# A sparse attention and feed-forward kernel: the first batch's feed-forward units pinned in traced order, at other rates, and its transposes one tile later

## The chip, the cores and the metric

The kernel runs on one core of a Trainium2 chip. The metric is the device time of one execution in microseconds (us); before the change the median of three runs is 1228.44 us (1227.75 to 1228.84). A core has five engines that work side by side, each on its own instructions in their fixed order: TensorE (PE in the profile) multiplies matrices and transposes, VectorE (DVE) and ScalarE (ACT) do element-wise work and reductions, GpSimd (POOL) more of that, and SyncE (SP) issues the transfers. A matrix product is accumulated in PSUM, a small memory of banks, from which DVE and ACT read it. TensorE's order comes from a list scheduler: the program is traced in Python, each instruction gets a priority by the place where it was traced, and for each engine the scheduler picks among the instructions that it believes ready.

## The reference

There are 8 batches of 8 heads, 576 positions, 64 values a head. Scores are thresholded at their row's maximum less tau, and the attention output feeds a two-layer unit with 512 inputs and 2048 hidden values.

```python
scores = scale * np.matmul(q, k.transpose(0, 1, 3, 2))
thresh = np.max(scores, axis=-1, keepdims=True) - tau
scores = np.where(scores >= thresh, scores, -1000000000.0)
attn = np.exp(scores - np.max(scores, axis=-1, keepdims=True))
attn = attn / (np.sum(attn, axis=-1, keepdims=True) + 1e-09)
x = np.matmul(attn, v)            # then heads side by side: 4608 rows of 512
h = x @ w_in
out = (h * (1.0 / (1.0 + np.exp(-h)))) @ w_out
```

## The kernel before

**Tiles.** Attention runs over tiles of 128 query rows. A tile's number t is in its names: `s_53` is the score tile 53 in PSUM, `w32_53` its weights, `hl_53` their split into a high and a low half-precision part. Batch 0 has tiles 0 to 15 (the first 256 rows of each head, "low") and 28 to 47 (the other 320 rows, "high"); numbers 16 to 27 are empty steps. Batch 1 has tiles 49 to 84, and from 85 on each batch has 36 tiles, up to 300. A tile goes through `scores` (TensorE, L452 in batch 0 and L464 later), `soft1` (DVE, row maximum, L474), `soft1b` (ACT, the exponential, L484), `soft2` (DVE, threshold and row sum, L493), `soft2b` (scaling by the sum: POOL at L507 in batch 0, ACT at L511 later) and `soft3`. The last differs. In batch 0, whose tiles stay in fp32, `soft3_direct` transposes five blocks on TensorE (L403 `tm`, L408 `tl`) and ACT copies them to `wT` (L416, L417). From batch 1 on POOL makes the two half-precision parts (L519, L522, L525), and a transfer transposes them (L535). When both heads of a pair have all tiles of a range in `wT`, `av_direct` (L426) or `av` (L550) multiplies by V, and `av_post` writes the result to `x16`.

**Buffers.** Two score tiles in PSUM, four `w32`, four `hl`, three `wT`. A `wT` buffer holds one head of one pair and range; batch 0 and the later batches share the three.

**Feed-forward units (FFN).** When a range of a batch is complete, `moe_units` adds its units to a list: 16 `h_unit`s (12 matmuls each, L593, then two steps on ACT and two on DVE at L601 to L609) and 16 quarters of `o_unit`s (12 matmuls each, L624; the fourth quarter of each writes its output by ACT and a transfer, L634 and L636). `h_0_256_3` is the fourth hidden block for batch 0 from row 256 on, `o_0_0_2` the third output block for batch 0 from row 0.

**What sets the order.** A loop over t traces the work of each step, with priorities for scores (`PRI_S`), the softmax and later AVs; `av_direct`, the loads and the units have none. A credit grows by `rate` at each step and pays for one unit of the list at a time. For batch 0 the rate is given by `RATES`; from batch 1 on it is the number of units on the list over the steps to the next range, times 0.95, so units left over from before are counted in. The weights are loaded, decoded and split on ACT, DVE and POOL during batch 0 (`W_PLAN`). Batch 1's V is scaled with a factor that goes through a small matmul on TensorE, `v1_ps`, traced at step 51 (L114 by way of `vscale`), before its first AV.

Of the kernel before, what the change touches and what calls it, by code (L numbers as in the profile page):

```python
# [30 lines left out]
LOAD = 5  # L31
AV_LAG = 3
GAP, GAP1 = 12, 1
RATES = (0.9, 0.9)
RATE = 0.95

W_PLAN = ((0, 0, 10, 13, 0), (16, 9, 22, 36, 0))
# [14 lines left out]
def attention_moe(  # L52
# [10 lines left out]
    nc = tc.nc  # L63
# [35 lines left out]
    for i in range(2):  # L99
        t = const.tile([P, S + 64], F32R, name=f"qstack{i}")  # L100
# [263 lines left out]
    direct = {}  # L364
    qzero = {}
    for kind, base, n in (("low", 4096, 256), ("high", 5120, 320)):
        for i in range(2):
            t = gbuf.bitcast(F32)[:, base + 2 * n * i : base + 2 * n * (i + 1)]
# [69 lines left out]
    tiles = []  # L438
# [74 lines left out]
    def soft3(t):  # L513
        if tiles[t][0] in direct:
            return soft3_direct(t)
        w = wtile.pop(t)
        hl = sb.tile([P, 9, P], F16, tag="hl", name=f"hl_{t}", bufs=4)
        fl = hl.rearrange("p j c -> p (j c)")
        nc.gpsimd.tensor_scalar(  # L519
            out=fl[:, 0:S], in0=w, scalar1=1.0, scalar2=1.0, op0=ALU.mult, op1=ALU.mult  # L520
        )
        nc.gpsimd.tensor_tensor(  # L522
            out=fl[:, 640:1152], in0=w[:, 0:512], in1=fl[:, 0:512], op=ALU.subtract
        )
        nc.gpsimd.tensor_tensor(  # L525
            out=fl[:, 576:640], in0=w[:, 512:576], in1=fl[:, 512:576], op=ALU.subtract
        )
        v, parts = tiles[t]
        kind = visits[v][2]
        base = VISITS[kind][2][0][0]  # L530
        for h, i, r0, n in parts:
            if (v, h) not in wT:
                wT[v, h] = sb.tile([P, 9, S], F16, tag="wT", name=f"wT_{v}_{h}", bufs=3)
            c = i * P - base
            nc.sync.dma_start_transpose(out=wT[v, h][:, :, c : c + n], in_=fl[r0 : r0 + n, :])  # L535
# [50 lines left out]
    def h_unit(b, c0, n, f, own=None):  # L586
        if f == 0:
            place_g(b, c0, n)
        ph = bank([P, 512], f"h_{b}_{c0}_{f}", own)
        k = 0  # L590
        for c in range(NK):
            for lo_w, lo_x in ((0, 0), (0, 1), (1, 0)):
                nc.tensor.matmul(  # L593
                    ph[:, :n], wi(c, f, lo_w), x16[b, lo_x][:, c, c0 : c0 + n],
                    start=(k == 0), stop=(k == 11),
                )
                k += 1

        def post():
            th = sb.tile([P, WID], F32, tag="th", name=f"th_{b}_{c0}_{f}", bufs=2)  # L600
            nc.scalar.activation(th[:, :n], ph[:, :n], AF.Tanh, scale=moe_sc[b][:, 0:1])  # L601
            nc.vector.scalar_tensor_tensor(  # L602
                out=ph[:, :n], in0=th[:, :n], scalar=1.0, in1=ph[:, :n],
                op0=ALU.add, op1=ALU.mult,
            )
            o = gbase[b, c0] + 2 * n * f
            g = gbuf[:, o : o + 2 * n].rearrange("p (r n) -> p r n", r=2)
            nc.scalar.activation(g[:, 0, :n], ph[:, :n], AF.Copy, scale=2.0**-14)  # L608
            nc.vector.scalar_tensor_tensor(  # L609
                out=g[:, 1, :n], in0=ph[:, :n], scalar=2.0**-14, in1=g[:, 0, :n],  # L610
                op0=ALU.mult, op1=ALU.subtract,
            )
            gt[b, c0, f] = g

        return post

    def o_unit(b, c0, n, d, quarter, own=None):
        if quarter == 0:
            po[b, c0, d] = bank([P, 512], f"o_{b}_{c0}_{d}", own)
        ps = po[b, c0, d]  # L620
        for f in range(4 * quarter, 4 * quarter + 4):
            g = gt[b, c0, f]
            for k, (lo_w, lo_g) in enumerate(((0, 0), (0, 1), (1, 0))):
                nc.tensor.matmul(  # L624
                    ps[:, :n], wo(f, d, lo_w), g[:, lo_g, :n],
                    start=(f == 0 and k == 0), stop=(f == NF - 1 and k == 2),
                )

        def post():
            if quarter < 3:  # L630
                return

            o = wst[:, NW + d % 2, :]
            nc.scalar.activation(o[:, :n], ps[:, :n], AF.Copy, scale=moe_sc[b][:, 1:2])  # L634
            c = b * S + c0
            nc.sync.dma_start(out=outT[d * P : (d + 1) * P, c : c + n], in_=o[:, :n])  # L636

        return post
# [34 lines left out]
    def at(t, f):  # L673
        todo.setdefault(t, []).append(f)

    avs = {}
    ready = []
    start = {}
    for v, (b, p, kind) in enumerate(visits):
        if b == 0 and kind == "high" and p == 0:  # L680
            tiles.extend([None] * GAP)
            first_high = len(tiles)
        if b == 1 and p == 0 and kind != "high":
            tiles.extend([None] * GAP1)
        ta, tb, ranges = VISITS[kind]
        u = len(tiles)
        start.setdefault((b, p), u)
        ha = b * H + 2 * p
        for i in ta:
            if i < 4:  # L690
                tiles.append((v, [(ha, i, 0, P)]))
            else:
                tiles.append((v, [(ha, 4, 0, D), (ha + 1, 4, D, D)]))
        last_a = len(tiles) - 1
        for i in tb:
            tiles.append((v, [(ha + 1, i, 0, P)]))
        last_b = len(tiles) - 1
        use_b = last_a if 4 in ta else last_a + 1
        if b == 0:
            at(u - LOAD, lambda v=v: load_direct(v))  # L700
            at(u - 2, lambda v=v: scale_direct(v))
            c0, n = ranges[0]
            avs.setdefault(last_b + AV_LAG, []).append((v, p, c0, n))
            if p == NPAIR - 1:
                ready.append((last_b + AV_LAG + 1, b, c0, n))
            continue
        for h, use, tl, last in ((ha, u, ta, last_a), (ha + 1, use_b, tb + [4] * (4 in ta), last_b)):
            at(use - LOAD, lambda v=v, h=h, tl=sorted(tl): load_qk(v, h, tl))
            at(use - 3, lambda h=h: split_k(h))
            at(use - 2, lambda h=h, tl=sorted(tl): split_q(h, tl))  # L710
        for j, (c0, n) in enumerate(ranges):
            avs.setdefault(last_b + AV_LAG + j, []).append((v, p, c0, n))
        if p == NPAIR - 1:
            for j, (c0, n) in enumerate(ranges):
                ready.append((last_b + AV_LAG + j + 2, b, c0, n))
# [63 lines left out]
    def live(t):  # L779
        return 0 <= t < NT and tiles[t] is not None  # L780

    scores(0)
    t = 0
    while t < NT + 8 or units or ready or held:
        while ready and ready[0][0] <= t:
            _, b, c0, n = ready.pop(0)
# [4 lines left out]
            if b == 0:  # L791
                rate = RATES[0 if c0 == 0 else 1]
        if held and not ready and not units and t >= NT + 8:
# [8 lines left out]
            soft2b(t - 1)  # L802
        if live(t):
            pri(PRI_SOFT1, lambda: soft1b(t))()
        if live(t - 1):
            soft3(t - 1)
        for f in todo.pop(t, []):
            f()
        credit += rate
# [7 lines left out]
        for v, p, c0, n in avs.pop(t, []):  # L817
            b = visits[v][0]
# [58 lines left out]
```

## Time and profile before

| | |
|---|---|
| three runs, median | 1228.44 us (1227.75 to 1228.84) |
| the profiled execution | 1225.66 us |
| its span | 1223.9 us |
| PE busy / weight loads | 1150.3 us (94%) / 899.2 us (73%) |
| DVE, ACT, POOL busy | 933.7, 796.4, 707.5 us |
| mean granted TensorE clock | 0.987 |
| matmuls of the FFN | 2 x 3072, 425.8 and 417.9 us busy |

The span is the time from the first to the last instruction; the execution's own time has 1.76 us around it. "Busy" is the time in which an engine works on at least one instruction; matmuls overlap, and their ends are modelled, so a busy TensorE is not one at its peak. A row of a group names line, engine, operation, what it writes and reads, its count, and its busy time and mean duration in ns; behind the last bar stands the engine's idle time ahead of it, and what ended that.

### The profile page before, as it was taken

Reading aid. Unit: us, or ns where it says so; the run is one execution under the profiler, and the core shown is the slowest. Engines: PE = TensorE matmul, PEld = TensorE weight load, DVE = VectorE, ACT = ScalarE, POOL = GpSimd, SP = SyncE. Lnnn points to the kernel's source line nnn. Section 1 sums busy time; section 2 is a strip of 40 time slices with the busy share of each in tenths; the row PEclk is TensorE's granted clock in tenths of the full one; section 3 lists DMA queues with packets and bytes.
Section 4 is the critical chain, followed back from the end, with each engine's and each line's share of the span. In section 5 each row is a group of like instructions: output and inputs, shape, how many; then the busy total and the mean of one; then the engine's idle time right before and its main releaser. Section 6 shows DMA issues by size and latency. Waiting matters only on the chain.

```text
span 1223.9 us, 27062 instructions
## 1 busy us (share of the span) xinstructions
PE 1150.3 (94%) x9474; PEld 899.2 (73%) x9474; DVE 933.7 (76%) x2625; ACT 796.4 (65%) x1505; POOL 707.5 (58%) x902
## 2 busy tenths in 40 slices
PE   6868799999899799999999999999999999999998
PEld 4545567777786577787777777788778877777777
DVE  7988988988999988889889858886788858333330
ACT  6667875876867777777777747785677756333331
POOL 2385357887877587886888428781778547100000
PEclk9979999999999999999999999999999999999999
DMA  9553148889788777886987448772877356200000
GB/s 309 185 161 95 41 108 173 160 160 177 132 177 141 160 137 139 150 165 151 167 149 145 114 94 155 146 136 82 153 150 142 77 92 116 42 11 16 16 10 25
DMA packets 340887, 151.73 MB, mean 124 GB/s; under 512 B 305936, under 2 KB 317200, under 8 KB 340752
## 3 DMA queue, kind: packets, MB, share of 16 engines
q1 hardware_dynamic: 340752, 150.01, 59.1%
q8 instruction: 75, 1.23, 0.4%
q14 instruction: 60, 0.49, 0.1%
HBM read 66.19 MB, written 9.44 MB: 62 GB/s over the span
## 4 chain that ended last, share of the span: by engine, by line
PE 63%; DVE 11%; DMA 10%; POOL 7%; issue 4%; ACT 4%; SPq 1%; POOLq 0%; ACTq 0%; DVEq 0%
PE o L624 24%; PE h L593 21%; PE s L464 9%; PE a L550 7%; DMA wT<-hl 4%; POOL hl L522 3%; DMA wraw<-in_w_out 3%; DVE w L493 2%; POOL hl L519 2%; DVE sm L474 2%; DVE qstack L350 2%; POOL hl L525 1%; DMA wraw<-in_w_in 1%; ACT w L484 1%; ACT w L511 1%
## 5 line engine op out<-in xcount | busy, mean ns | idle before, releaser
L593 PE MATMUL h<-x,wst 128*128 128x288 f16 (+2 forms) x3072 | 425.8, 288 | 7.8 <-DVE gbuf L609 5.0
L624 PE MATMUL o<-gbuf,wst 128*128 128x288 f16 (+2 forms) x3072 | 417.9, 286 | 2.4 <-ACT wst L634 2.4
L593 PEld LDWEIGHTS <-wst 128*128 128x128 f16 x3072 | 292.2, 98 | 95.7 <-issue 16.9
L624 PEld LDWEIGHTS <-wst 128*128 128x128 f16 x3072 | 292.7, 98 | 83.7 <-issue 7.4
L522 POOL TENSOR_TENSOR hl<-w,hl 128x512 f16<-128x512 f32 x252 | 302.6, 1201 | 12.8
L519 POOL TENSOR_SCALAR hl<-w 128x576 f16<-128x576 f32 x252 | 172.2, 686 | 193.4 <-ACT w L511 115.7
L484 ACT ACTIVATE w<-s,sm 128x576 f32<-128x576 f32 x288 | 211.6, 739 | 91.9 <-DVE sm L474 39.1
L493 DVE SCALAR_TENSOR_TENSOR w<-s,sm,w 128x576 f32<-128x576 f32 x288 | 232.0, 812 | 39.9 <-ACT w L484 37.8
L474 DVE TENSOR_REDUCE sm<-s 128x1 f32<-128x576 f32 x288 | 214.4, 749 | 28.7 <-PE s L464 21.8
L511 ACT ACTIVATE w<-w,sm 128x576 f32<-128x576 f32 x252 | 191.4, 771 | 52.1 <-DVE sm L501 50.1
L602 DVE SCALAR_TENSOR_TENSOR h<-th,h 128x288 f32<-128x288 f32 (+2 forms) x256 | 116.2, 455 | 113.7 <-ACT th L601 112.3
L601 ACT ACTIVATE th<-h,msc 128x288 f32<-128x288 f32 (+2 forms) x256 | 126.6, 498 | 103.2 <-PE h L593 101.8
L464 PE MATMUL s<-khi,qstack 128*128 128x288 f32 x560 | 144.3, 338 | 12.7 <-DVE w L493 9.9
L608 ACT ACTIVATE gbuf<-h 128x288 f16<-128x288 f32 (+2 forms) x256 | 104.3, 408 | 78.2 <-DVE h L602 77.5
L609 DVE SCALAR_TENSOR_TENSOR gbuf<-h,gbuf 128x288 f16<-128x288 f32 (+2 forms) x256 | 115.3, 452 | 41.9 <-ACT gbuf L608 41.0
L550 PE MATMUL a<-wT,v 128*64 128x288 f16 (+2 forms) x1568 | 115.0, 289 | 10.8 <-DMA wT<-hl 10.6
L360 POOL TENSOR_TENSOR klo<-kraw,khi 128x576 fp32r<-128x576 f32 x64 | 94.5, 1476 | 47.1 <-ACT khi L358 47.0
L464 PE MATMUL s<-klo,qstack 128*128 128x288 f32 x560 | 120.8, 296 | 0.0
L464 PEld LDWEIGHTS s<-khi,qstack 128*128 128x128 f32 x560 | 87.7, 190 | 31.9 <-issue 15.4
L550 PEld LDWEIGHTS <-v 128*64 128x64 f16 x1568 | 84.5, 110 | 33.7 <-issue 22.1
L464 PEld LDWEIGHTS s<-klo,qstack 128*128 128x128 f32 x560 | 90.4, 189 | 0.6
L525 POOL TENSOR_TENSOR hl<-w,hl 128x64 f16<-128x64 f32 x252 | 89.5, 355 | 0.0
(101 smaller groups left out, 930.4 us busy)
## 6 DMA issues: line engine op xcount, KB each, us to landing
kraw<-in_kT SPq DMA_DIRECT2D x128, 144.0 KB, 3.0
qraw<-in_qT SPq DMA_DIRECT2D x96, 144.0 KB, 3.0
vraw<-in_vL SPq DMA_DIRECT2D x32, 320.0 KB, 3.6
wraw<-in_w_out SPq DMA_DIRECT2D x16, 512.0 KB, 3.7
out_t<-wst SPq DMA_DIRECT2D x48, 144.0 KB, 2.1
wT<-hl SPq DMA_TRANSPOSE x280, 3.4
gbuf<-in_w_in SPq DMA_DIRECT2D x8, 512.0 KB, 6.2
wraw<-in_w_in SPq DMA_DIRECT2D x8, 512.0 KB, 5.1
```

What stands on the lines that cost most here:

```text
L464: nc.tensor.matmul(s_ps[:, j, :HALF], lhs, kk[:, j * HALF : (j + 1) * HALF], start=(n == 0), stop=(n == len(seq) - 1),)
L474: nc.vector.tensor_reduce(out=negm, in_=s_ps[:, :, :HALF], op=ALU.max, axis=AX.XY, negate=True)
L484: nc.scalar.activation(wtile[t].rearrange("p (j c) -> p j c", j=2), sps[t][:, :, :HALF], AF.Exp, bias=small[t][:, 0:1],)
L493: nc.vector.scalar_tensor_tensor(out=w3, in0=s_ps[:, :, :HALF], scalar=sm[:, 1:2], in1=w3, op0=ALU.is_ge, op1=ALU.mult, accum_out=sm[:, 2:3],)
L511: nc.scalar.activation(w, w, AF.Copy, scale=r)
L519: nc.gpsimd.tensor_scalar(out=fl[:, 0:S], in0=w, scalar1=1.0, scalar2=1.0, op0=ALU.mult, op1=ALU.mult)
L522: nc.gpsimd.tensor_tensor(out=fl[:, 640:1152], in0=w[:, 0:512], in1=fl[:, 0:512], op=ALU.subtract)
L550: nc.tensor.matmul(a_ps[odd * D : (odd + 1) * D, :n], vt[:, lo_v, odd, kv, :], wT[v, b * H + 2 * p + odd][:, kw, c0 - base : c0 - base + n ...
L593: nc.tensor.matmul(ph[:, :n], wi(c, f, lo_w), x16[b, lo_x][:, c, c0 : c0 + n], start=(k == 0), stop=(k == 11),)
L601: nc.scalar.activation(th[:, :n], ph[:, :n], AF.Tanh, scale=moe_sc[b][:, 0:1])
L602: nc.vector.scalar_tensor_tensor(out=ph[:, :n], in0=th[:, :n], scalar=1.0, in1=ph[:, :n], op0=ALU.add, op1=ALU.mult,)
L624: nc.tensor.matmul(ps[:, :n], wo(f, d, lo_w), g[:, lo_g, :n], start=(f == 0 and k == 0), stop=(f == NF - 1 and k == 2),)
```

## The change

`RATES` goes from 0.9 and 0.9 units a step to 1.03 for batch 0's first range and 1.45 for its second. The first matmul of each unit of batch 0 is pinned behind the TensorE instruction that was traced just ahead of it: the scheduler may not issue it earlier, though later work may still pass it. In batch 0 `soft3_direct` is traced at step t + 2 instead of t + 1, its AVs one step later, and its two ranges become ready one step later (20 and 52 in place of 19 and 51). Below stands the diff; lines of the new kernel are three to seven higher than those of the old one from L593 on.

```diff
-RATES = (0.9, 0.9)
+PACED = 1
+RATES = (1.03, 1.45)
...
-                nc.tensor.matmul(
+                mm = nc.tensor.matmul(
                     ph[:, :n], wi(c, f, lo_w), x16[b, lo_x][:, c, c0 : c0 + n],
                     start=(k == 0), stop=(k == 11),
                 )
+                if b < PACED and k == 0:
+                    tc.keep_in_program_order(mm)
...
-                nc.tensor.matmul(
+                mm = nc.tensor.matmul(
                     ps[:, :n], wo(f, d, lo_w), g[:, lo_g, :n],
                     start=(f == 0 and k == 0), stop=(f == NF - 1 and k == 2),
                 )
+                if b < PACED and f == 4 * quarter and k == 0:
+                    tc.keep_in_program_order(mm)
...
-            avs.setdefault(last_b + AV_LAG, []).append((v, p, c0, n))
+            avs.setdefault(last_b + AV_LAG + 1, []).append((v, p, c0, n))
             if p == NPAIR - 1:
-                ready.append((last_b + AV_LAG + 1, b, c0, n))
+                ready.append((last_b + AV_LAG + 2, b, c0, n))
...
-        if live(t - 1):
+        if live(t - 1) and tiles[t - 1][0] not in direct:
             soft3(t - 1)
+        if live(t - 2) and tiles[t - 2][0] in direct:
+            soft3(t - 2)
```

In the built program the order moves most where batch 0 hands over to batch 1. First TensorE around score tile 53, before. `v1_ps` is the small matmul for batch 1's V factor, `a_0_3_256` batch 0's last AV, which reads the two `wT` buffers `wT_7_6` and `wT_7_7`, and `o_0_0_0` the first output block.

```order
L114 MATMUL v1_ps_2073<-v1_diag_2071,ones_91 128x128
L408 MATMUL tl_47_1954<-ident_93,w32_47_1912 128x128
L464 MATMUL s_53_2109<-khi_10_2013,qstack0_85 128x288 x2
L464 MATMUL s_53_2109<-klo_10_2015,qstack0_85 128x288 x2
...
L426 MATMUL a_0_3_256_2038<-wT_7_6_1787,vraw_0_3_117 64x320
L426 MATMUL a_0_3_256_2038<-wT_7_7_1880,vraw_0_3_117 64x320
...
L464 MATMUL s_54_2151<-khi_10_2013,qstack0_85 128x288 x2
L464 MATMUL s_54_2151<-klo_10_2015,qstack0_85 128x288 x2
L624 LDWEIGHTS wst_89
L624 MATMUL o_0_0_0_1535<-gbuf_61,wst_89 128x256
```

After the change the same two stand behind nearly all of the four output blocks, eight tiles further on:

```order
L465 MATMUL s_60_2550<-khi_13_2386,qstack1_87 128x288 x2
L465 MATMUL s_60_2550<-klo_13_2388,qstack1_87 128x288 x2
...
L115 MATMUL v1_ps_2099<-v1_diag_2097,ones_91 128x128
L627 LDWEIGHTS wst_89
L627 MATMUL o_0_0_3_1983<-gbuf_61,wst_89 128x256
...
L427 MATMUL a_0_3_256_2128<-wT_7_6_1847,vraw_0_3_117 64x320
L427 MATMUL a_0_3_256_2128<-wT_7_7_1936,vraw_0_3_117 64x320
...
L594 MATMUL h_0_256_0_2170<-x16_0_0_475,wst_89 128x320
...
L551 MATMUL a_1_0_0_2335<-wT_8_9_2158,v16_1_0_2204 64x256
```

So the last AV of batch 0 and the factor for batch 1 moved from tiles 52 and 53 to tile 60; the output blocks that were traced ahead of them stay ahead.

Second, SP's queue at the same place, before: the transposing transfers of tiles 51 to 53 stand around the first of the four output transfers.

```order
L535 DMA_TRANSPOSE wT_8_9_2120<-hl_51_2116 128x9x128
L250 DMA vraw_2_1_2210<-in_vL 128x640
L250 DMA vraw_2_2_2647<-in_vL 128x640
L535 DMA_TRANSPOSE wT_8_9_2120<-hl_52_2158 128x9x128
L334 DMA kraw_11_14_2319<-in_kT 64x576 x2
L335 DMA qraw_11_14_2318<-in_qT 64x256
L636 DMA out_t<-wst_89 128x256
L535 DMA_TRANSPOSE wT_9_10_2198<-hl_53_2194 128x9x128
```

And after, where the transfer of tile 51 stands behind the last of the four:

```order
L641 DMA out_t<-wst_89 128x256
L335 DMA kraw_12_9_2747<-in_kT 64x576
L336 DMA qraw_12_9_2746<-in_qT 64x320
L251 DMA vraw_2_0_1850<-in_vL 128x640
L536 DMA_TRANSPOSE wT_8_9_2158<-hl_51_2154 128x9x128
L536 DMA_TRANSPOSE wT_8_9_2158<-hl_52_2197 128x9x128
L536 DMA_TRANSPOSE wT_9_10_2243<-hl_53_2239 128x9x128
L251 DMA vraw_2_1_2255<-in_vL 128x640
L536 DMA_TRANSPOSE wT_9_10_2243<-hl_54_2307 128x9x128
```

Tile 51's transposing transfer writes the second of the three `wT` buffers that batch 1 needs, and batch 0's last AV still reads two of them; it moved behind that AV, and with it all later ones on SP's queue. Counted over the whole of TensorE's order, these many FFN matmuls stand ahead of a tile's scores:

| ahead of the scores of tile | 49 | 53 | 61 | 77 | 104 | 128 | 160 | 210 | 216 |
|---|---|---|---|---|---|---|---|---|---|
| before | 144 | 192 | 362 | 576 | 1037 | 1356 | 1877 | 2681 | 3002 |
| after | 156 | 192 | 420 | 675 | 1135 | 1442 | 1964 | 2788 | 3002 |

## Prediction

> **What bounds the kernel now.** I began with the page's totals.
>
> ```profile
> span 1223.9 us, 27062 instructions
> PE 1150.3 (94%) x9474; PEld 899.2 (73%) x9474; DVE 933.7 (76%) x2625; ACT 796.4 (65%) x1505; POOL 707.5 (58%) x902
> ```
>
> TensorE is the candidate, but a share over the whole span is a mean over stages. So the second view was the busy time by stretch (start:end, length, then busy us and instructions of PE, PEld, DVE, ACT, POOL, granted clock, DMA share, GB/s), cut where the tiles change phase.
>
> ```profile
> 0.00:57.00 57.00, 42.92 (x261) 28.54 (x262) 47.88 (x151) 36.98 (x71) 14.79 (x28) 0.97 0.76 246
> 57.00:107.00 50.00, 35.66 (x199) 22.54 (x196) 41.60 (x103) 33.36 (x68) 41.51 (x42) 0.83 0.52 164
> 107.00:174.00 67.00, 56.45 (x376) 41.07 (x377) 57.24 (x162) 49.92 (x113) 20.93 (x23) 0.95 0.19 50
> 174.00:204.00 30.00, 29.28 (x255) 23.57 (x254) 27.66 (x74) 19.21 (x34) 22.68 (x27) 1.00 0.77 179
> 204.00:256.00 52.00, 47.37 (x404) 36.49 (x403) 47.49 (x138) 42.76 (x84) 44.10 (x56) 1.00 0.82 162
> 256.00:290.00 34.00, 32.89 (x268) 24.77 (x267) 26.70 (x70) 21.64 (x35) 28.56 (x37) 1.00 0.93 174
> 290.00:347.00 57.00, 52.82 (x468) 44.04 (x465) 54.38 (x159) 42.70 (x80) 44.77 (x56) 1.00 0.76 153
> 347.00:426.00 79.00, 69.13 (x583) 53.05 (x581) 73.29 (x200) 58.41 (x106) 56.73 (x74) 0.98 0.84 161
> 426.00:695.00 269.00, 264.37 (x2231) 209.61 (x2231) 237.95 (x703) 201.11 (x364) 212.27 (x274) 1.00 0.76 145
> 695.00:735.00 40.00, 40.00 (x360) 31.62 (x359) 24.06 (x52) 19.98 (x40) 10.65 (x15) 1.00 0.50 105
> 735.00:1055.00 320.00, 313.84 (x2740) 251.94 (x2738) 250.48 (x726) 218.31 (x403) 210.53 (x277) 1.00 0.65 122
> 1055.00:1224.00 169.00, 165.56 (x1352) 132.00 (x1350) 44.95 (x100) 52.06 (x114) 0.00 (x0) 1.00 0.05 16
> ```
>
> TensorE idles 73.6 us in all. Of that 39.0 us lie before 174 us, and 20.5 us between 174 and 426 us (0.7, 4.6, 1.1, 4.2 and 9.9). From 426 us on it idles 14.2 us in 798. From there TensorE sets the pace: FFN work done early is not done again, and the end moves by it. Before 174 us DVE has 146.7 of 174 us, with the weights' decoding; between 204 and 426 us DVE has 91% and TensorE 91%, each waiting for the other.
>
> To place the tiles I read the DVE maximum of each tile (one per tile, 288 in all), asking for those from a time on.
>
> ```profile
> L474 DVE TENSOR_REDUCE sm<-s x248: 733/748/759, 173.7 to 1037.8; 128x1 f32<-128x576 f32 x124
> L474 DVE TENSOR_REDUCE sm<-s x173: 737/748/759, 426.4 to 1037.8; 128x1 f32<-128x576 f32 x173
> L474 DVE TENSOR_REDUCE sm<-s x86: 737/749/759, 697.8 to 1037.8; 128x1 f32<-128x576 f32 x86
> L474 DVE TENSOR_REDUCE sm<-s x85: 737/749/759, 731.8 to 1037.8; 128x1 f32<-128x576 f32 x85
> ```
>
> 248 are left from tile 53 on, so tile 53 is at 173.7, tile 128 at 426.4, tile 215 at 697.8 and tile 216 at 731.8: a hole of 34.0 us in the attention. In it TensorE was full (40.00 of 40.00), on backlog:
>
> ```profile
> 699.63 1.84 PE a L550 x28
> 701.47 5.99 PE o L624 x48
> 1131.02 2.94 PE h L593 x24
> 250.39 3.27 PE h L593 x24
> ```
>
> These rows of the chain of waits also price an AV of a later batch (1.84 us) and an FFN matmul: 2.94/24 = 0.1225 us with 288 columns, 0.136 with 320, 5.99/48 = 0.125.
>
> **The change, part by part.** *Batch 0's own stage (to tile 53).* The table of counts has 192 FFN matmuls ahead of tile 53 before and after: the units run in number order and one or two earlier, no more. The stall that pinning could end there is this one.
>
> ```profile
> PE h L593 <- DVE gbuf L609: 5.0, 7, 1.4
> ```
>
> It is a unit that waits for a bank which an earlier unit still holds; 5.0 us are the upper end of the gain. The stage's end hangs on weights, though: ACT decodes the last of 16 tiles of w_out at 107.38, and DVE's work is unchanged.
>
> ```profile
> 60.02 12.72 POOL L225 TENSOR_SCALAR wst<-wst,i_w_sc 128x512 f32<-128x512 f32 x16 [2.51 <-DVE i_w_sc L145]
> 107.38 0.69 ACT wst L190
> ```
>
> POOL's block of 16 splits now stands ahead of tile 13's scaling too, not only of 14's, and with transposes a tile later each `w32` is held longer. At worst a tile's step is lost, 6.2 us where that stretch has eight tiles in 50 us; at best the 5.0 us are won. I take 0, with the weight loads up to 107 us as cover; without that cover it is the 6.2 us.
>
> *Tiles 53 to 60.* TensorE is full here before (29.28 of 30.00), so 58 more FFN matmuls (420 against 362) push tile 61 back by 58 x 0.122 = 7.1 us: a lead in FFN work, paid in full. What is new is the wait. Tile 51's transfer needs a `wT` buffer that `a_0_3_256` frees, now eight tiles later. Four `hl` and four `w32` let tiles through 58 pass; tile 59's exponential waits. Behind the AV stand, in turn: the transfer to landing, POOL's three steps, the exponential, DVE's threshold.
>
> ```profile
> L535 SPq DMA_TRANSPOSE wT<-hl x280: 1199/1302/2502, 167.7 to 1045.1; - x140
> DMA to landing us min/median/max: 2.8/3.4/5.3
> L522 POOL TENSOR_TENSOR hl<-w,hl 128x512 f16<-128x512 f32 x252 | 302.6, 1201 | 12.8
> L519 POOL TENSOR_SCALAR hl<-w 128x576 f16<-128x576 f32 x252 | 172.2, 686 | 193.4 <-ACT w L511 115.7
> L525 POOL TENSOR_TENSOR hl<-w,hl 128x64 f16<-128x64 f32 x252 | 89.5, 355 | 0.0
> L484 ACT ACTIVATE w<-s,sm 128x576 f32<-128x576 f32 x288 | 211.6, 739 | 91.9 <-DVE sm L474 39.1
> L493 DVE SCALAR_TENSOR_TENSOR w<-s,sm,w 128x576 f32<-128x576 f32 x288 | 232.0, 812 | 39.9 <-ACT w L484 37.8
> ```
>
> 3.4 + 2.24 + 0.74 + 0.81 = 7.2 us until tile 61's scores may start. TensorE has 36 FFN matmuls (36 x 0.136 = 4.9 us) and the AV `a_1_0_0` (1.84 us) to cover it: 6.7 us. I take 0.5 us exposed; bounds 0 and 4 (landing at 5.3, and two more transfers at 1.3 each ahead of the AV's second half). That a wait of this kind is otherwise covered, the present kernel shows: POOL stood still longest for such a transfer just where TensorE was full.
>
> ```profile
> POOL hl L519 <- DMA wT<-hl: 56.7, 6, 23.7
> 725.16 0.67 POOL L519 TENSOR_SCALAR hl<-w 128x576 f16<-128x576 f32 x1 [23.70 <-DMA wT<-hl]
> ```
>
> *Tiles 61 to 76 (204 to 256 us before).* The lead grows from 58 to 99 matmuls, 41 x 0.136 = 5.6 us more TensorE work against 4.6 us of idle. DVE is not in the way: of the 16 `h` posts three have moved ahead of tile 61, and three of seven query splits. At 0.91 us a post (455 and 452 ns) and 0.9 us a query split, that takes 5.4 off its 47.5 us.
>
> ```profile
> L602 DVE SCALAR_TENSOR_TENSOR h<-th,h 128x288 f32<-128x288 f32 (+2 forms) x256 | 116.2, 455 | 113.7 <-ACT th L601 112.3
> L609 DVE SCALAR_TENSOR_TENSOR gbuf<-h,gbuf 128x288 f16<-128x288 f32 (+2 forms) x256 | 115.3, 452 | 41.9 <-ACT gbuf L608 41.0
> L350 DVE SCALAR_TENSOR_TENSOR qstack<-qraw,gate,qstack 64x256 fp32r<-64x256 f32 x8 | 7.2, 896 | 2.3 <-ACT qstack L349 2.2
> L312 DVE SCALAR_TENSOR_TENSOR v<-vraw,v_sc,v 128x640 f16<-128x640 f32 x28 | 29.2, 1063 | 0.4 <-ACT v L311 0.4
> ```
>
> So the idle can be filled; from none of it to all 4.6 us, and I take 4.
>
> *Tiles 77 to 127.* The lead stays (98 at tile 104, 86 at tile 128), and the work per tile is the same. The 15.2 us of idle at 256 to 426 us are of DVE's bunches (73.29 of 79 us in the last stretch, with the V splits of two batches): they recur, or fall otherwise. The ends are -5 and +4 us; between them I take 1 us won: in DVE's order 16 posts in place of 17 stand between tiles 104 and 128.
>
> *From tile 128 on.* 86 matmuls are 10.5 us of lead, 107 at tile 210 are 13.1 us, none is left at tile 216 (3002 both). It must be given back in the hole: 34.0 - 13.1 = 21 us there. Nothing is won or lost here, since TensorE is full.
>
> **The sum**: 0 + 0.5 - 4 - 1 = -4.5 us. The span goes from 1223.9 to 1219.4 us, the profiled execution from 1225.66 to 1221.2, and the median, 2.78 us above that execution, from 1228.4 to 1224.
>
> [...]
>
> **Rivals.**
>
> *A dearer handover (slower).* DVE has little to do between tiles 57 and 60: no posts, and the four V splits of batch 1 wait for `v1_ps`. Behind it DVE's order has those four (4 x 1.06 us), three query splits (3 x 0.9), a row maximum of V and two posts ahead of tile 59's threshold, some 9 us, in which each V split also waits for its copy by ACT. If these waits double the bunch, 9 us lie bare where TensorE's cover of 6.7 us has run out, and DVE, then as full as TensorE, can't make them up before tile 77: +9 + 0.5 - 4 = +5.5 us, 1234 us. It decides from the point where the bunch lasts longer than the 7.2 us in which tile 59 waits for its transfer anyway. For it: DVE at 47.49 of 52 us right behind. Against it: the bunch starts with `v1_ps`, twelve matmuls and an AV earlier than that wait.
>
> *Given back (same).* The lead is pushed into the attention one for one everywhere, TensorE's 4.6 us stay as other waits: 1228 us. For it: DVE and TensorE both at 91% between 204 and 426 us.
>
> *More idle goes (faster).* The bunch at 347 to 426 us, 9.9 us, dissolves too since tiles and FFN meet differently: 1215 us.
>
> *The clock.* A stall costs more than its length where the granted clock falls:
>
> ```profile
> 147.75 2.50 PE L593 MATMUL h<-x,wst 128*128 128x256 f16 x12 [1.07 <-DVE gbuf L609]
> 153.32 1.47 PE L593 MATMUL h<-x,wst 128*128 128x256 f16 x12
> ```
>
> The same unit took 2.50 us behind a stretch of short waits and 1.47 us later, so a stall at tile 61 adds about 1 us; this is in the bounds above. [...]
>
> *The change does not do what it says.* For batch 0's first range that is nearly so (192 and 192 at tile 53); for the second range the counts rule it out.
>
> **How the numbers follow.** The forecast's case 45%, with a range of its own of 1219 to 1227; more idle goes 15%; given back 20%; the dearer handover 20%. What this kernel's measurement can tell from no change is about 0.2%, 2.5 us. The forecast's case ends faster by that in about four of five, and else within it (0.36 and 0.09); given back splits into 0.14 within and 0.06 slower. With the 0.15 of more idle, and the 0.20 of the handover: faster 0.51, same 0.23, slower 0.26. The range takes in most of both outer cases: 1211 to 1236.
>
> **What would show it.** Right: tile 53 within 3 us of 173.7; tile 61 some 7 us later than before (it is near 204 there); TensorE idle between tiles 61 and 77 down from 4.6 to about 1 us; tile 128 at 430 to 434 us; the hole ahead of tile 216 down from 34 to about 21 us. Wrong: POOL waiting for a transposing transfer around tile 55 with TensorE idle for over 4 us beside it, tile 128 later than 437 us (then the whole lead of 10.5 us was paid for), or tile 53 late by more than 4 us.

## The result, and the profile after

The changed kernel takes 1235.82 us (median of 6 runs, 1234.11 to 1241.65) against 1228.48 us before: a ratio of 1.0072, 95% interval 1.0053 to 1.0090. It is slower. Measured once more (e5) it was 1238.75 against 1229.22 us, 1.0066 (1.0042 to 1.0089).

The totals of the changed kernel's page come first.

```profile
span 1235.1 us, 27047 instructions
...
PE 1164.6 (94%) x9474; PEld 906.9 (73%) x9474; DVE 932.4 (75%) x2625; ACT 799.8 (65%) x1505; POOL 705.2 (57%) x902
```

TensorE idles 70.5 us, 3.1 less than before, and is busy 14.3 us longer with the same 9474 matmuls. The mean granted clock fell from 0.987 to 0.978. So the loss isn't a larger sum of waits: the same matmuls take longer, at a lower clock. Where? Below is the busy time by stretch (columns as in the prediction), cut at tiles 15, 53, 60, 61, 77, 128, 160, 168, 208, 216 and 300:

```profile
0.00:71.30 71.30, 54.66 (x288) 35.69 (x289) 52.77 (x170) 41.53 (x81) 17.54 (x31) 0.86 0.67 218
71.30:176.60 105.30, 85.63 (x546) 61.18 (x546) 92.40 (x244) 77.75 (x170) 56.58 (x59) 0.90 0.31 95
176.60:199.30 22.70, 22.70 (x203) 20.31 (x201) 17.07 (x50) 15.05 (x27) 15.64 (x19) 1.00 0.38 101
199.30:216.20 16.90, 14.69 (x113) 10.25 (x111) 12.69 (x31) 9.94 (x19) 7.39 (x10) 0.90 0.71 165
216.20:272.10 55.90, 53.16 (x438) 39.96 (x437) 45.32 (x138) 40.94 (x77) 44.76 (x58) 1.00 0.80 161
272.10:439.90 167.80, 155.87 (x1311) 122.30 (x1310) 149.61 (x425) 121.95 (x219) 130.13 (x167) 0.99 0.81 159
439.90:541.00 101.10, 98.84 (x836) 77.51 (x833) 91.77 (x266) 77.72 (x143) 79.89 (x104) 1.00 0.77 148
541.00:574.70 33.70, 30.88 (x251) 24.04 (x251) 29.27 (x76) 22.00 (x39) 22.10 (x28) 0.95 0.76 158
574.70:695.75 121.05, 120.08 (x1037) 95.96 (x1036) 107.61 (x311) 91.67 (x167) 97.84 (x127) 1.00 0.77 148
695.75:739.30 43.55, 40.27 (x351) 32.04 (x349) 33.46 (x93) 27.07 (x51) 19.53 (x25) 1.00 0.51 118
739.30:1047.10 307.80, 303.14 (x2594) 240.65 (x2590) 247.62 (x712) 213.99 (x390) 207.79 (x274) 0.99 0.65 124
...
```

Before, tiles 160 to 168 took 23.0 us with TensorE never idle:

```profile
527.50:550.50 23.00, 23.00 (x203) 18.31 (x198) 20.90 (x66) 17.42 (x32) 19.84 (x26) 1.00 0.88 155
```

Three things stand out: a clock of 0.86 up to tile 15 (0.97 before), 16.9 us between tiles 60 and 61 (0.8 before), and 33.7 us for tiles 160 to 168, at 0.95. Much of the lower clock lies ahead of tile 53 (0.88 up to there, 0.92 before), and yet tile 53 comes only 2.9 us later than before, so the clock alone doesn't place the loss. And a tile that is late may only have more FFN work ahead of it. So I kept a **ledger**: a tile's lag behind the first profile of the kernel before (by its row maximum on DVE), less the TensorE work that the order has ahead of its scores beyond that kernel's. That work is priced from rows: FFN matmuls at 0.109, 0.1225 and 0.136 us (256, 288, 320 columns), an AV at 1.84 us, an fp32 one at 3.0, a transpose at 0.17 and any other small matmul at 0.10. At tile 61 the changed kernel lags by 12.6 us; the 58 FFN matmuls more account for 7.0 of them, and the ledger says 5.6. What rises in it is lost.

| tile | before, again | changed | changed, again | e10 RATE 1.0 | e12 V's scale 4 | e6 paced | e15 best | e15 again (e18) |
|---|---|---|---|---|---|---|---|---|
| 15 | 1.1 | 10.0 | 10.2 | 4.5 | 6.1 | 0.0 | 0.7 | 0.0 |
| 53 | 2.6 | 3.0 | 6.9 | -0.7 | 0.9 | -2.7 | -4.7 | -3.6 |
| 60 | 2.3 | 0.6 | 4.5 | -3.1 | -1.5 | -4.6 | -4.5 | -5.3 |
| 61 | 2.3 | 5.6 | 9.4 | 1.9 | 3.6 | 1.9 | -4.5 | -5.3 |
| 65 | 2.5 | 1.3 | 5.3 | -2.3 | -0.5 | 2.0 | -6.7 | -8.0 |
| 77 | 2.6 | 2.7 | 7.8 | -0.7 | 0.8 | 0.5 | -5.7 | -3.4 |
| 104 | 3.1 | 1.6 | 6.5 | -2.4 | -0.4 | 1.5 | -7.7 | -5.5 |
| 128 | 3.3 | 2.1 | 6.9 | -1.4 | 0.5 | 3.8 | -7.7 | -5.0 |
| 160 | 2.8 | 2.4 | 8.9 | -1.4 | 0.6 | 1.9 | -10.1 | -7.5 |
| 168 | 3.2 | 7.7 | 13.2 | -0.2 | 0.8 | 7.4 | -9.0 | -6.4 |
| 208 | 3.3 | 5.0 | 10.6 | -3.5 | 2.4 | 3.4 | -11.9 | -7.2 |
| 216 | 3.4 | 7.5 | 13.1 | -3.5 | 2.4 | 3.5 | -11.1 | -6.3 |
| 300 | 3.9 | 11.2 | 15.1 | -2.1 | 4.3 | 5.1 | -14.9 | -5.7 |

The second profile of the kernel before (e11) gives a first scale: two profiles differ by 2.6 us up to tile 53, in the weights' stage, and by 1.4 us more in all that follows. Other pairs differ more. The two of the changed kernel are 3.9 us apart at tile 53 and 3.8 to 6.5 behind it; the two of e15 are 1.0 apart at tile 53 and 9.2 at tile 300. So only a rise that comes back in several profiles counts here. The four profiles with the changed order up to tile 104 (the changed kernel twice, e10 and e12) go alike from 53 on: 5 us are lost at tile 61, 4 of them are back by tile 65, and at tile 104 they stand 0.4 to 1.7 us lower than at tile 53. Up to there this order has lost nothing for good. Behind tile 104 the changed kernel loses 9.6 and 8.7 us, e10 0.3 and the kernel before, again, 0.9. That is about the whole of the result's 7 to 10 us.

### The profile page after: what moved, and what is told of

It is laid out like the page before. It is cut to its first block, busy times and chain, and to the rows that moved or that the text cites. A ratio compares the mean times of both kernels' runs of the same rounds, so it can differ in the third digit from the quotient of the medians.

```text
span 1235.1 us, 27047 instructions
## 1 busy us (share of the span) xinstructions
PE 1164.6 (94%) x9474; PEld 906.9 (73%) x9474; DVE 932.4 (75%) x2625; ACT 799.8 (65%) x1505; POOL 705.2 (57%) x902
## 4 chain that ended last, share of the span: by engine, by line
PE 59%; DVE 18%; DMA 7%; ACT 6%; issue 5%; POOL 3%; SPq 1%; ACTq 0%; POOLq 0%; DVEq 0%
PE o L627 22%; PE h L594 19%; PE s L465 8%; PE a L551 6%; DVE w L494 5%; DVE sm L475 3%; DMA wT<-hl 3%; DVE qstack L351 3%; PE s L453 2%; ACT w L485 2%; DVE v L313 1%; PE a L427 1%; DVE h L605 1%; ACT w L512 1%; DMA wraw<-in_w_out 1%
## 5 line engine op out<-in xcount | busy, mean ns | idle before, releaser
L594 PE MATMUL h<-x,wst 128*128 128x288 f16 (+2 forms) x3072 | 421.1, 287 | 6.3 <-DVE gbuf L612 6.3
L465 PE MATMUL s<-khi,qstack 128*128 128x288 f32 x560 | 144.7, 339 | 13.1 <-DVE w L494 10.8
L551 PE MATMUL a<-wT,v 128*64 128x288 f16 (+2 forms) x1568 | 120.7, 292 | 9.9 <-DMA wT<-hl 9.6
L361 POOL TENSOR_TENSOR klo<-kraw,khi 128x576 fp32r<-128x576 f32 x64 | 91.9, 1435 | 59.8 <-ACT khi L359 55.2
```

Of the source, the lines that this page charges most:

```text
L465: nc.tensor.matmul(s_ps[:, j, :HALF], lhs, kk[:, j * HALF : (j + 1) * HALF], start=(n == 0), stop=(n == len(seq) - 1),)
L551: nc.tensor.matmul(a_ps[odd * D : (odd + 1) * D, :n], vt[:, lo_v, odd, kv, :], wT[v, b * H + 2 * p + odd][:, kw, c0 - base : c0 - base + n ...
L594: mm = nc.tensor.matmul(ph[:, :n], wi(c, f, lo_w), x16[b, lo_x][:, c, c0 : c0 + n], start=(k == 0), stop=(k == 11),)
```

## The experiments

Kernels are compared with the kernel before on the same chip; "ratio" is to that, with its 95% interval.

**The three parts, each alone.** e1: the change's `RATES`. e2: its pinning. e3: its later transposes, AVs and readiness.

```diff
e1  -RATES = (0.9, 0.9)          +RATES = (1.03, 1.45)
e2  +PACED = 1    +if b < PACED and k == 0: tc.keep_in_program_order(mm)    (and the same for o)
e3  -soft3(t - 1) for every tile    +soft3(t - 2) where tiles[t - 2][0] in direct
    -AV_LAG, AV_LAG + 1             +AV_LAG + 1, AV_LAG + 2
```

> The kernel before with RATES (1.03, 1.45) alone. Its TensorE order is that of the kernel before until about tile 85, and from there the units fall otherwise among the tiles (1963 FFN matmuls ahead of tile 160, as in the changed kernel, against 1877; 2904 ahead of tile 215 against 2769). Handover theory (the 7.3 us are lost at tile 61, where V's scale and the last AV of batch 0 stand behind output blocks): nothing is moved at tile 61, so 1228.5 us within 2. Scatter theory (the loss comes from tile 128 on, where units, V splits and batch boundaries meet in another order): tile 128 within 3 us of before, and then 3 to 6 us lost, 1231.5 to 1234.5 us.

> The kernel before with batch 0's units pinned and nothing else. V's scale for batch 1 and the last AV of batch 0 stay at tile 52, and units come later than before (296 FFN matmuls ahead of tile 61 against 362), so that 66 x 0.122 = 8 us of TensorE work are missing ahead of tile 61. Handover theory: no hole at tile 61; within 3 us of 1228.5. Scatter theory: 1229 to 1233 us, lost from tile 77 on. A third theory (a stall that pinning makes: a pinned unit waits for a bank or a weight and later work of the same engine stands behind it): tile 53 late by over 4 us and the span longer by that.

> The kernel before with batch 0's transposes, AVs and readiness one step later and nothing else. The last AV of batch 0 stands at tile 58 (before 53, changed kernel 60), V's scale at tile 57. Handover theory: a hole ahead of tile 61 is back, with at least 3 of the 5.7 us that the changed kernel lost net of its FFN lead; 1232 to 1235 us. Scatter theory: no more at tile 61 than the lead of 31 matmuls (3.8 us); what is lost comes after tile 128; 1229 to 1234 us. If the loss of some 10 us net at tiles 15 to 41 in the changed kernel is the transposes' (each fp32 tile held a step longer), it is seen here at tile 15 too.

Measured: e1 1225.92 us, 0.9981 (0.9963 to 0.9999); e2 1229.28, 1.0002 (0.9984 to 1.0020); e3 1231.94, 1.0026 (1.0005 to 1.0046). The parts add up to 0.1%, the whole is 0.7%: no part carries the loss alone. e1 fits neither theory, being a little faster; its rates do nothing ahead of tile 85, since the scheduler puts unpinned units where it likes. In e2, 66 FFN matmuls fewer stand ahead of tile 61, some 8 us, but the tile comes only 1.5 us earlier: its ledger goes from -4.8 at tile 53 to 4.9 at tile 61, and is back at 1.3 by tile 216. e3's tile 61 lost nothing (4.5 to 4.1 net), so the handover theory's "at least 3" was wrong there. Its late transposes do show early: tile 15 stands at 11.2 (its profile is the slowest of its twelve runs), and at 4.5 to 10.2 in the four profiles of the changed order, against 0.0 to 1.1 where transposes are early. On TensorE, the kernel before (first fence) issues tile 6's scores ahead of most of the first fp32 AV. The changed kernel (second) issues them behind most of it, and there an fp32 matmul takes 0.30 us in place of 0.16, at a granted clock of 0.51 in place of 0.89:

```profile
25.73 2.29 PE L452 MATMUL s<-kd,gbuf 128*128 128x288 f32 x4
27.95 2.79 PE L426 MATMUL a<-wT,vraw 128*64 128x256 f32 x18
```

```profile
29.19 4.72 PE L427 MATMUL a<-wT,vraw 128*64 128x256 f32 x16 [0.58 <-ACT wT L417]
33.84 1.24 PE L453 MATMUL s<-kd,gbuf 128*128 128x288 f32 x4
```

**The handover at tile 61.** e4 puts both V's scale for batch 1 and batch 0's last AV of the changed kernel back to tile 53, e7 only the first, e8 only the second. e6 is the change without the later transposes.

```diff
e4, e7  -lambda b=b: vscale(b))
        +lambda b=b: pri(PRI_AV * (b == 1), lambda: vscale(b))())
e4, e8  -a_ps = av_direct(v, p)
        +a_ps = pri(PRI_AV * (v == 7), lambda v=v, p=p: av_direct(v, p))()
e6  e1 and e2 together
```

> The changed kernel, with V's scale for batch 1 and the last AV of batch 0 given the priority that later AVs have: both come back to tile 53, as in the kernel before, behind 192 FFN matmuls; units stay pinned and at the new rates, and tiles stay transposed a step later. Handover theory: the 16.9 us between tiles 60 and 61 shrink to those of the FFN work, tile 61 loses under 2 us net of its lead in place of 5.7, and the time is 1229 to 1232 us. Scatter theory: tile 61 is won, but the end is not (or by chance): 1232 to 1238 us, with new losses where the units now meet batches 2 to 5.

> The kernel before with batch 0's units pinned and at the new rates; tiles are transposed as before. As in the changed kernel 420 FFN matmuls stand ahead of tile 61, the last AV of batch 0 at tile 59 and V's scale at tile 60. Handover theory: the hole at tile 61 is there (12 us or more), 4 to 6 us net of the FFN work, and the time is 1232 to 1236 us though nothing is transposed later. Transposes theory (the loss is that of holding each fp32 tile a step longer, which alone cost 3.3 us, with a lower clock): no more than 2 us net at tile 61, and 1227 to 1230 us.

> The changed kernel with V's scale for batch 1 alone given the priority of later AVs, which puts it back to tile 53; the last AV of batch 0 stays behind the output blocks, at tile 59. If the hole at tile 61 is the bunch of V splits on VectorE behind V's scale, it shrinks from 16.9 us to under 8 us. If it is the AV, whose buffer the first transfer waits for, it stays at 12 us or more. The time goes with it: 1230 to 1232 us, or 1234 to 1236 us.

> The changed kernel with the last AV of batch 0 alone given the priority of later AVs, which puts it back to tile 53; V's scale for batch 1 stands at tile 61, behind tile 60. If the hole is the AV's, tiles 60 and 61 are under 8 us apart and the scores go on. If it is V's scale, the hole stays or moves to where four hl buffers are full and the transfers stand behind V's load on SP's queue: 10 us or more between two of the tiles 58 to 64. Times as in the run beside it, the other way round.

Measured: e4 1234.69 us, 1.0044 (1.0023 to 1.0065); e6 1231.96, 1.0024 (1.0004 to 1.0044); e7 1236.19, 1.0059 (1.0035 to 1.0084); e8 1239.91, 1.0080 (1.0052 to 1.0108). From tile 60 to 61 the ledger rises by nothing in e4 and by 6.5 us in e6. In e7 the hole stays, 12.3 us between tiles 60 and 61, as it should if it is the AV's, and the ledger rises by 3.6. In e8 tiles 60 and 61 are 2.9 us apart, but 4.9 us are lost between 63 and 65. So both belong to the hole: with either of the two late there is one. e8 fits its two cases by half (the longest gap, 9.6 us, is between 63 and 64) and is slower than both gave. And e4, with no hole, was only 0.3% under the changed kernel, its interval overlapping that one's, as the scatter theory had it: in the changed kernel the hole isn't where the 0.7% went. With early transposes it isn't made good: e6 stands 6.1 us higher at tile 104 than at tile 60.

The chain inside it, from the changed kernel's timelines (TensorE; SyncE's queue, with one of its waits; POOL, ACT and DVE):

```profile
200.88 3.06 PE L427 MATMUL a<-wT,vraw 128*64 128x320 f32 x20
203.87 5.06 PE L594 MATMUL h<-x,wst 128*128 128x320 f16 x36
211.14 3.11 PE L551 MATMUL a<-wT,v 128*64 128x256 f16 x28 [2.21 <-DMA wT<-hl]
214.18 0.75 PE L465 MATMUL s<-khi,qstack 128*128 128x288 f32 x2
```

```profile
204.62 1.52 SPq L251 DMA_DIRECT2D vraw<-in_vL  x1
206.25 4.21 SPq L536 DMA_TRANSPOSE wT<-hl  x3
...
SPq L251 <- DVE v L313: 1.6, 1, 1.6
```

```profile
203.66 3.27 DVE L313 SCALAR_TENSOR_TENSOR v<-vraw,v_sc,v 128x640 f16<-128x640 f32 x4 [0.51 <-ACT v L312]
...
210.13 0.67 POOL L520 TENSOR_SCALAR hl<-w 128x576 f16<-128x576 f32 x1 [8.85 <-DVE h L605]
...
212.34 0.74 ACT L485 ACTIVATE w<-s,sm 128x576 f32<-128x576 f32 x1 [2.96 <-POOL hl L526]
...
213.11 0.82 DVE L494 SCALAR_TENSOR_TENSOR w<-s,sm,w 128x576 f32<-128x576 f32 x1 [2.63 <-ACT w L485]
```

The fp32 AV ends at 203.9, but the transfer that waited for its buffer is issued only at 206.25: it stands in SP's queue behind loads, the last of them a load of V that waits 1.6 us for a buffer which a V split on DVE frees. Then come POOL's steps, the exponential, the threshold and the scores, 10.3 us after the AV. TensorE has 5.06 us of FFN work meanwhile. The AV behind it waits for a transfer too, with TensorE idle for 2.21 us, and then takes 3.11 us. An AV of its shape took 1.72 us in the kernel before (first line). The granted clock is 0.53 around the slow one (second line):

```profile
204.71 1.72 PE L550 MATMUL a<-wT,v 128*64 128x256 f16 x28 [0.42 <-DMA wT<-hl]
...
211.10:214.20 3.10, 3.06 (x29) 2.71 (x29) 1.09 (x3) 1.81 (x4) 3.10 (x5) 0.53 1.08 234
```

**Second profiles.** e5 is the changed kernel, e11 the kernel before, unedited.

> The changed kernel once more, for a second profile and for a direct comparison with the three beside it. Handover theory: the hole of 16.9 us between tiles 60 and 61 is there again within 2 us, and it is the first place at which the kernel falls behind for good. Scatter theory: the hole is there, but what is lost at tiles 160 to 168 and 208 to 230 (5 us each in the first profile, net of FFN work) is lost at other places or not at all; 1233 to 1237 us by both.

> The kernel before once more, for a second profile: how far two profiles of one kernel differ tile by tile. If the ledger by tiles can be trusted, differences stay within 2 us at tiles 61, 128, 160 and 216 after what lies in the weights' stage ahead of tile 53 is taken off; the time is 1228.5 us within 1.

The hole is there again (16.9 us), and so are the losses at 160 to 168 (4.3 us, and 5.4 in the first profile) and from 208 on (4.5 us to tile 300, and 6.2): they are of the order and not of one execution. e11 ran at 1230.14 us, 1.0000 (0.9978 to 1.0022).

**Behind tile 104.** e10 is the changed kernel and e14 the kernel before, each with another RATE for batches 1 to 7. e12 and e13 move V's scale of the changed kernel, for batch 4 and for batches 4 and 5.

```diff
e10, e14  -RATE = 0.95    +RATE = 1.0
e12  -(1, u + 2)[b] if b < 2 else u - 2
     +(1, u + 2)[b] if b < 2 else u - 2 + 4 * (b == 4)
e13  +(1, u + 2)[b] if b < 2 else u - 2 + 4 * (b in (4, 5))
```

> The changed kernel with RATE 1.0 in place of 0.95. Its TensorE order is the changed kernel's through tile 104; from there the units fall a little otherwise (1930 FFN matmuls ahead of tile 160 against 1964), and V's scale for batch 4 stands at tile 166 in place of 161, that for batch 5 at 212 in place of 208. Scatter theory: the hole at tile 61 is there as before, the stall at tiles 160 to 168 (5 us net in both profiles of the changed kernel) is gone, and 3 to 5 us are won: 1232 to 1235 us against 1237. If what is lost lies ahead of tile 104 (handover and transposes alone), the time stays within 2 us of the changed kernel's.

> The changed kernel with V's scale for batch 4 traced four steps later: TensorE's order is the changed kernel's through tile 160, and then this one small matmul stands at tile 167 in place of 161, and units fill its place. Theory of V's splits (behind V's scale stand four V splits on VectorE, ahead of the thresholds of tiles 162 to 165): the stall at tiles 160 to 168, 5 us net of TensorE's work in both profiles of the changed kernel, shrinks to 1.5 us or less, and at least 3 us stay won at tile 208. Theory of the units (FFN posts on VectorE and the filled TensorE make the stall): it stays at 4 us or more. As V's scale for batch 5 stands at tile 205 here, earlier still than 208, 208 to 216 may lose more than the 2.5 us of before; so 1231 to 1236 us by the first theory, 1235 to 1239 by the second.

> As the run beside it, with V's scale for batch 5 four steps later too (tile 211). Theory of V's splits: the stalls at 160 to 168 and at 208 to 216 are both under 2 us net, 5 to 8 us are won in all, 1229 to 1232 us. Theory of the units: 1235 to 1239 us.

> The kernel before with RATE 1.0. Its order is that of the kernel before through tile 85, then that of RATES alone at 0.95 through tile 160 (1963 FFN matmuls ahead), with V's scale for batch 4 at tile 163 and for batch 5 at 210. If the changed kernel is slower only where it meets RATE 0.95, the two kernels at RATE 1.0 are within 3 us of each other, this one at 1223 to 1229 us. If RATE 1.0 is simply better and the change costs 0.7% at any rate, this one runs at 1216 to 1219 us.

Measured: e10 1225.45 us, 0.9964 (0.9948 to 0.9980); e12 1231.19, 1.0021 (1.0010 to 1.0033); e13 1231.19, 1.0024 (1.0001 to 1.0046); e14 1222.75, 0.9955 (0.9938 to 0.9972). e10 has the hole (5.0 us) and the early stage, and is faster than the kernel before; it missed both of its cases, the nearer of which gave 1232 us. At RATE 1.0 the changed kernel and the kernel before differ by 0.1% by the two ratios; at 0.95 by 0.7%.

e12 changes no TensorE instruction up to tile 160, and then one small matmul's place (tile 167 for 161), for which units trade places. The ledger's rise between tiles 160 and 168 goes from 5.4 (4.3 again) to 0.3, and in e13 to 0.3 too. Cut at those tiles, e12 shows TensorE without idle, as before the change:

```profile
539.20:564.70 25.50, 25.50 (x226) 20.75 (x226) 20.61 (x67) 19.05 (x35) 20.91 (x28) 1.00 0.92 159
```

A V split (L313) is the step on DVE that makes the second half-precision part of V, after ACT's copy has made the first. In the changed kernel, DVE has three of batch 4's V splits, and a wait for ACT's copy, between the row maximum of tile 162 (547.86) and its threshold (554.46); TensorE, whose next scores need that threshold, idles for 2.05 us. Behind that wait the granted clock is 0.50 for 3.4 us, and the 24 FFN matmuls there take 4.78 us. In the second profile (e5) the wait is there again (1.92 us), but the clock stays at 1.00 and the same 24 take 3.11 us. The changed kernel's rows, the last one a stretch:

```profile
549.80 1.81 DVE L313 SCALAR_TENSOR_TENSOR v<-vraw,v_sc,v 128x640 f16<-128x640 f32 x1 [0.93 <-ACT v L312]
551.53 0.74 DVE L475 TENSOR_REDUCE sm<-s 128x1 f32<-128x576 f32 x1
552.20 2.22 DVE L313 SCALAR_TENSOR_TENSOR v<-vraw,v_sc,v 128x640 f16<-128x640 f32 x2
...
554.46 0.80 DVE L494 SCALAR_TENSOR_TENSOR w<-s,sm,w 128x576 f32<-128x576 f32 x1
...
555.42 0.51 PE L465 MATMUL s<-khi,qstack 128*128 128x288 f32 x2 [2.05 <-DVE w L494]
556.03 4.78 PE L627 MATMUL o<-gbuf,wst 128*128 128x288 f16 x24
...
556.00:559.40 3.40, 3.40 (x16) 2.15 (x15) 3.40 (x10) 0.82 (x2) 0.00 (x0) 0.50 0.81 184
```

So that stall is V's scale, and it is shown: with this one matmul moved the ratio is 1.0021 in place of 1.0072 and 1.0066, with intervals that don't meet. The tile alone doesn't fix the size, though: with the scale at tile 161 as well, e6 loses 5.4 us there but e1 only 2.5, and e1 is faster than the kernel before. At tile 200 e12 is 4.6 us better off against tile 160 than the changed kernel (-1.8 and 2.8). It keeps less than the expected 3 us by tile 208, since batch 5's scale has come forward to tile 205 and 3.6 us are lost between 200 and 208. The changed kernel, with that scale at tile 208, loses 2.5 us between 208 and 216 in both profiles, e13 (211) 1.6 and e10 (212) none. That speaks for the same cause, but the differences are small and it is not shown. What is lost from tile 216 to 300 isn't settled: 3.7 and 2.0 us in the changed kernel, 3.5 in e13, 1.9 in e12, 1.4 in e10 and 0.5 in the second profile of the kernel before.

**What wins, and whether it adds.** e9 is e6 (no later transposes) with e4's two lines; e15 is e9 with RATE 1.0, and e18 that once more. e16 is e4, and e17 e6, with RATE 1.0.

```diff
e9   e6, and the two lines of e4
e15, e18  e9 and RATE = 1.0        e16  e4 and RATE = 1.0        e17  e6 and RATE = 1.0
```

> The kernel before with batch 0's units pinned and at the new rates, tiles transposed as before, and V's scale for batch 1 and the last AV of batch 0 given the priority of later AVs (they stand at tiles 53 and 55). Theory of three terms (pinning and the new rates win about 5 us until tile 60, the handover at tile 61 gives 5 to 7 back, transposes a tile later cost about 5): only the first is left here, so no hole at tile 61, tile 61 ahead of the kernel before net of its TensorE work by 2 to 5 us, and 1223 to 1227 us. If it is schedule scatter from tile 77 on that decides, it is as likely at 1232 as at 1224 us.

> Pinned units, the new rates, tiles transposed as before, V's scale for batch 1 and the last AV of batch 0 early, and RATE 1.0. Through tile 85 it is the kernel of the run with RATE 0.95, which stood 5 to 7 us ahead of the kernel before there, net of its work, and lost 4 of them between 104 and 140 and 3 at 160 to 168. If those losses are of the order there, this other order keeps part of them: 1219 to 1224 us. If an early lead is always lost by the end of the attention, as DVE sets the pace in between: 1225 us again.

> The changed kernel with V's scale for batch 1 and the last AV of batch 0 early and with RATE 1.0 (tiles still transposed a step later). If the handover at tile 61 is a lasting loss of its own (it seemed worth 4 us at RATE 0.95 with late transposes and 7 us without), 1219 to 1222 us against 1225.5 with the hole. If the hole is made good by tile 77 and those gains were of the order behind it, 1223 to 1228 us.

> Pinned units at the new rates with RATE 1.0, tiles transposed as before, and the last AV of batch 0 and V's scale for batch 1 behind the output blocks (tiles 59 and 60), so with the hole at tile 61. If transposes a tile later are worth 5 to 7 us for good, 1218 to 1221 us (1225.5 with both). If the hole is worth as much, 1220 to 1222 us against 1215 without it; if neither lasts, 1214 to 1217 us.

> The fastest kernel once more: 1213 to 1217 us, 0.9 to 1.3% below the kernel before, with TensorE idle for 60 to 64 us in all against 73 in the kernel before.

| median us (ratio) | RATE 0.95 | RATE 1.0 |
|---|---|---|
| before | 1228.7 | 1222.75 (0.9955) |
| changed: late transposes, late handover | 1235.8, 1238.75 (1.0072, 1.0066) | 1225.45 (0.9964) |
| late transposes, early handover | 1234.69 (1.0044) | 1231.96 (1.0017) |
| early transposes, late handover | 1231.96 (1.0024) | 1232.73 (1.0026) |
| early transposes, early handover | 1225.28 (0.9978) | 1215.04, 1217.57 (0.9887, 0.9888) |

The interval of e9 is 0.9960 to 0.9997, of e15 0.9867 to 0.9907, of e18 0.9862 to 0.9914, of e16 1.0000 to 1.0033, of e17 1.0011 to 1.0041. e15 beats both kernels by over 1%. e15 was faster, and e16 and e17 slower, than every theory gave them. At RATE 0.95 an early handover wins 1 to 4 us with late transposes and 7 without, at 1.0 it loses 6.5 with late ones and wins 15 to 18 without. RATE itself is worth between -13 and +1 us by the row. No part has a price of its own in these runs. The likely reason is that each part shifts where units, V splits and batch boundaries meet for 200 tiles; beyond the stall at tiles 160 to 168 that is not shown. e18 came out half a microsecond above what was expected, with TensorE idle for 65.6 us, 1.6 above it. e15 has pinning's early win (tile 53 at -4.7), no hole, and 1.2 us lost at tiles 160 to 168. Its ledger falls all the way to -14.9, but this profile is the fastest of its six runs; e18's, the slowest of its six, ends at -5.7. In e15's, TensorE idles 62.0 us in all:

```profile
span 1209.0 us, 27049 instructions
...
PE 1147.0 (95%) x9474; PEld 898.2 (74%) x9474; DVE 926.4 (77%) x2625; ACT 797.8 (66%) x1505; POOL 705.4 (58%) x902
```

## Why the prediction was wrong

It forecast 1224 us and faster; it is 1235.8 and slower, just inside the upper end of the range.

*From tile 128 on*, "Nothing is won or lost here, since TensorE is full", is the step that failed. The mean over 269 us (264.37 busy) hid that single stretches had no reserve. From tile 128 to 300 the two profiles of the changed kernel lose 9.1 and 8.2 us, and the second one of the kernel before 0.6. Of these, 5.4 and 4.3 us are lost at tiles 160 to 168, where V's scale for batch 4 came six tiles earlier, at 161 and not 167: a wait of TensorE for DVE, and in the first profile a granted clock of 0.50 behind it. Then 2.8 and 2.6 us are given back by tile 208, perhaps because the kernel before has batch 4's V splits there (tiles 168 and 169). The prediction looked at V's scale for batch 1 alone. No rival named this. What is lost from tile 216 on stays open.

*The handover, 0.5 us (bounds 0 and 4)*, was mis-sized: 5.0 and 4.9 us by the ledger from tile 60 to 61. The chain was named rightly, link by link, but it took 10.3 us for 7.2: SP's queue adds 2.4 us ahead of its first link. And of the 6.7 us of cover, 1.84 were the AV `a_1_0_0`, which itself waits for such a transfer; the FFN's 5.06 were all.

*Tiles 61 to 76, -4 us*: TensorE's waits between 61 and 65 did go (3.3 us before, none after), but they only paid for the hole; between 65 and 77, 1.4 and 2.5 us are lost. With the handover's 0.5 the prediction had -3.5 from tile 60 to 77; it is +2.1 and +3.3.

*Batch 0's stage, 0 us (-5.0 to +6.2)*: right as a sum. At tile 60 the four profiles of this order stand at 0.6, 4.5, -3.1 and -1.5, two of the kernel before at 0 and 2.3. It was two ends at once: pinned at the new rates alone stands at -2.7 to -4.7 at tile 53, and the later transposes bring it back. *Tiles 77 to 127, -1 us*: -0.6 and -0.9, right. At tile 128 the sum was to stand at -4.5 us; the changed kernel stands at 2.1 and 6.9 there, the kernel before at 0 and 3.3.

*What would show it*: tile 53 came 2.9 us later (right), tile 61 12.6 and not 7, idle between 61 and 77 was 2.7 and not 1, the hole ahead of tile 216 16.1 us and not 21. Tile 128 at 439.9 us crossed the mark that was to mean that the whole lead was paid for, and so it was: 13.6 us later than before, 11.5 of them the lead (most of its 86 matmuls have 320 columns; the prediction's 10.5 prices 288) and 2.1 more. What made the kernel slower came later.

*The rivals*: the dearer handover's 1234 us is nearest, and its mechanism is half right: V splits behind `v1_ps` do hold up the chain, by way of SP's queue. But the 9 us that DVE was not to make up before tile 77 were 5, and 4 of them were made up by tile 65. It has the right time for a reason that isn't the reason. *Given back* holds up to tile 104.

The clock: the AV behind the 2.21 us wait took 3.11 us and not 1.72, 1.4 us more, near what the clock rival said (1 us), though the two rows it compares are two units of one shape and not one unit twice. The granted clock was 0.53 over the slow AV and 1.00 over the one of the kernel before (204.70 to 206.40); over the prediction's two rows it was 0.55 (147.75 to 150.25) and 1.00 (153.32 to 154.80). That a wait lowers the clock, and from which length on, no run shows: 2.21 us stood ahead of 0.53 here, and 1.92 us ahead of 1.00 in the second profile.

## What to carry to other kernels

Before you call a local stall the cause, take the work that was moved off each lag and see whether the stall is still there a few tiles on. Where a list scheduler sets the order, one constant far from the change (here `RATE`) can move the time more than the change does, so compare both versions at several of its values before you keep or drop the change. Count an instruction as cover only if it doesn't wait for the same queue as what it is to cover.

## What was not expected of the hardware

Two executions of one order differ by several microseconds: the profiles of the kernel before by 2.6 us up to tile 53, at granted clocks of 0.987 and 0.983 (spans of 1223.9 and 1227.8 us), and those of e15 and e18 by 8.2 us behind it, at 0.993 and 0.989 (1209.0 and 1218.3). Over the 35 runs beside e1 to e4 the kernel before takes 1224.0 to 1234.4 us, with clocks of 0.987 and 0.979 at the ends: run-to-run differences of 0.8% go with the clock, which has a mean of 0.986 over the 17 fastest of them and of 0.982 over the 17 slowest. Waits of TensorE of 2.05 and 2.21 us in the changed kernel's first profile each stood ahead of some 3 us at a granted clock of 0.50 and 0.53, while one of 1.92 us in its second stood ahead of 1.00. Behind the wait of 2.05 us 24 FFN matmuls took 4.78 us, behind the one of 1.92 us the same 24 took 3.11, 1.67 us less. And a transposing transfer whose data and buffer were ready was issued 2.4 us late because loads stood ahead of it in SP's queue, one of them waiting for DVE.
